# Tile loads on one DMA queue, tables on another, groups of 8, 7 and 9 tiles, and a conversion in five stages

## Chip, cores and metric

One core of one Trainium2 chip. The metric is the device time in microseconds (us) of one execution of the whole program.

## What is computed

Three parts follow each other on 3072 tokens of 512 features.

```python
for t in range(S):                                   # attention: B=4, H=8, S=768, D=64
    state = gamma * state + k[t] outer v[t]          # per batch and head, 64x64
    y[t] = scale * q[t] @ state
logits = x @ w_gate                                  # mixture of 8 experts, one per token
e = argmax(logits)
out = softmax(logits)[e] * sigmoid(x @ w_output_gate)[e] * (relu(x @ w1[e]) @ w2[e])   # 512 -> 1024 -> 512
h = x @ w_in                                         # dense part: 512 -> 2048 -> 512
out = (h - tanh(h)) @ w_out
```

All inputs are float32, but `w_in` and `w_out` reach the kernel as float64 (pairs of 32-bit words) and are converted on the chip. The matrix products of the experts and of the dense part are made of three products each: every float32 operand x is split into a rounded part `hi` and a rest `lo = x - hi`, and hi*hi, hi*lo, lo*hi are added.

## The kernel before, in words

The instructions are written in the order in which each engine runs them; the tile framework only adds the waits. So the order of the work is the order of the calls below, engine by engine, and an instruction that waits holds up all behind it on its engine or its DMA queue.

**Attention and gating** (loop over `n`, lines 914 to 995). 24 tiles of 128 tokens, six per batch. `load(n)` (L586) brings q, k, v of a tile (1 MB) by DMA; tiles 0 to 2 and 6 on are issued on SP, tiles 3, 4 and 5 on ScalarE's queue (ACT). Tables (`ca`: masks, powers and indices; `cb`: identity and indices; `wgs`: gate weights; `qt[1]`) come on SP between the first loads. At tile 6's load four stores of `lead` and one of `far` fill the pads of two DRAM tensors. Loads run up to five tiles ahead, from six buffers, later three tiles ahead from four. Per tile: `attend(n)` (L655: state, outputs `o`, on TensorE; copies `st`, `xT` on ACT), `scores(n + 2)` (L617: products `sc`, masked on VectorE as `pt`; `qd`, `kd` on GpSimd), `rows(n)` (L705: transposes `tr`, copies `xr` on ACT, row sums `lp` on VectorE, and a store of `xr` to the DRAM tensor `xtok`, issued on ACT).

Tiles form three groups of eight. At a group's end VectorE picks each token's expert (`onehot`), TensorE counts ranks (`ranks`), VectorE writes for each tile a mark of 432 columns (`ohr`, L799) and computes gates (`scale`); these short operations wait in lists, `scales` and `convs`, and `fill` (L325) lets a budget of 2.6 (an estimate in us) of them onto VectorE per tile, each costed at 0.2 if it names no other figure. `slots` (L853) then gathers the places of tokens by products `ip`. After the second group, `head` (L864) gathers the first 216 tokens of expert 0 from the tiles so far; so steps of that expert can begin as attention ends.

**Conversion of float64** (`conv_m`, L264). A piece is half of one of 16 blocks of weights, 128x512 values: ACT copies the high words (`keep`), VectorE makes exponent and mantissa (`ta`, `va`, five operations, v0 to v4), ACT rounds to `hi`, GpSimd subtracts for `lo` (L308). 32 pieces in all; four (NPA) are converted in attention through the list `convs`, 28 in the places of the experts. Blocks 12 to 15 (NRES on) go back to DRAM (`dh`, `dl`) and are read again in the last stage.

**Experts** (place 0 from L1003, the other places in the loop at L1099). Nine places: two halves of expert 0 (216 tokens each), then seven experts in the order of their counts, with 432, 420, 408, 400, 388, 380 and 368 columns. Each place has eight steps `i`: `mm1` (L417, TensorE product `ph`, then `hi` on ACT and `lo` on VectorE) and `mm2` of the step before (L434, product `ya`). The weights of the next step (`wr`, 0.5 MB by SP, three buffers) are split into `wh` on ACT and `wl`, by `conv_w` (L231): part 0, for `mm1`, on VectorE in odd steps and on GpSimd in even ones, part 1, for `mm2`, on VectorE. Tokens of the next place are gathered by GpSimd (`gather`), scaled by ACT (`weigh`) and transposed and split (`turn`, `split`: `xt`, `xh`, `xl`), in steps 6 and 7 of a place, two transposed blocks in each. One slot of the conversion falls into most steps: a slot with the third stage of piece j - 1 (ACT `hi`, GpSimd subtraction) and the first of piece j (ACT `keep`, VectorE v0 to v2), then a slot with the second of piece j (v3, v4).

**Last stage.** Six blocks of 512 tokens (`fetch2`, `split2`: DMA `x2r` from DRAM, `x2h` on ACT, `x2l` on GpSimd; block 0's are issued in the last place), 16 steps each of `mm3` and `mm4` (L1200, L1214).

## Time and profile before

| | us |
|---|---|
| median of 3 runs | 1029.43 |
| lowest and highest of them | 1029.24, 1035.13 |
| the profiled execution | 1026.86 |
| its span, first to last instruction | 1025.1 |
| TensorE busy in the span | 972.1 |

The profile is of one execution. PE is TensorE's products, PEld its weight loads, DVE VectorE, ACT ScalarE, POOL GpSimd, SP the engine that only issues DMAs; a q behind an engine's name (ACTq) is its sequencer, which issues DMAs and waits. L308 is line 308 of the kernel. A tile's name stands left of the arrow where it is written and right of it where it is read. A bracket at a line's end is the idle time of the engine before that instruction and what ended it. The granted clock is that of TensorE, 1.00 for 2.4 GHz.

### The profile page before, as it was taken

Reading aid. Unit: us, or ns where it says so; the run is one execution under the profiler, and the core shown is the slowest. Engines: PE = TensorE matmul, PEld = TensorE weight load, DVE = VectorE, ACT = ScalarE, POOL = GpSimd, SP = SyncE. Lnnn points to the kernel's source line nnn. Section 1 sums busy time; section 2 is a strip of 40 time slices with the busy share of each in tenths; the row PEclk is TensorE's granted clock in tenths of the full one; section 3 lists DMA queues with packets and bytes.
Section 4 is the critical chain, followed back from the end, with each engine's and each line's share of the span. In section 5 each row is a group of like instructions: output and inputs, shape, how many; then the busy total and the mean of one; then the engine's idle time right before and its main releaser. Section 6 shows DMA issues by size and latency. Waiting matters only on the chain.

```text
span 1025.1 us, 16478 instructions
## 1 busy us (share of the span) xinstructions
PE 972.1 (95%) x5938; PEld 837.6 (82%) x5938; DVE 744.6 (73%) x1181; ACT 604.0 (59%) x1090; POOL 379.1 (37%) x333
## 2 busy tenths in 40 slices
PE   6899788999999999999999999999999999999995
PEld 4778678898989898999888888888888888888884
DVE  2387775778787788674987777777777777777772
ACT  2444342555565655554877767676676767767662
POOL 3276433243343353322342343243334325333322
PEclk9899998999999999999999999999999999999998
DMA  9899534476666675675300010010001001000001
GB/s 331 286 370 336 197 108 127 143 231 194 206 197 202 188 244 180 217 229 157 131 22 11 11 52 14 9 52 21 11 14 50 22 1 52 11 1 21 21 1 44
DMA packets 44011, 120.70 MB, mean 118 GB/s; under 512 B 9638, under 2 KB 15014, under 8 KB 41106
## 3 DMA queue, kind: packets, MB, share of 16 engines
q1 hardware_dynamic: 35170, 97.23, 29.1%
q0 software_dynamic: 4864, 12.91, 3.9%
q10 hardware_dynamic: 3888, 9.44, 2.4%
q8 instruction: 48, 0.79, 0.3%
q14 instruction: 41, 0.34, 0.1%
HBM read 95.99 MB, written 23.57 MB: 117 GB/s over the span
## 4 chain that ended last, share of the span: by engine, by line
PE 78%; DVE 9%; issue 4%; DMA 4%; ACT 2%; POOL 2%; SPq 0%; ACTq 0%; POOLq 0%; DVEq 0%
PE mh L1200 26%; PE ma L1214 26%; PE ph L427 9%; PE ya L451 9%; PE tr L716 2%; PE sc L631 1%; DMA x2c<-lead 1%; DVE ta L278 1%; DVE va L281 1%; PE o L690 1%; DVE wl L239 1%; DMA xtok<-xr 1%; DVE pt L624 1%; POOL wl L239 1%; DMA ld<-in_qkv 1%
## 5 line engine op out<-in xcount | busy, mean ns | idle before, releaser
L1182 POOL TENSOR_TENSOR gl<-g,gh 128x512 fp32r<-128x512 f32 x96 | 124.1, 1293 | 343.7 <-ACT gh L1181 341.1
L1200 PE MATMUL mh<-x2h,ml 128*128 128x512 f32 x384 | 151.6, 395 | 0.0
L1214 PE MATMUL ma<-ml,gh 128*128 128x512 f32 x384 | 151.6, 395 | 0.0
L1200 PE MATMUL mh<-x2h,mh 128*128 128x512 f32 x384 | 151.6, 395 | 0.0
L1214 PE MATMUL ma<-mh,gl 128*128 128x512 f32 x384 | 151.3, 394 | 0.0
L1214 PE MATMUL ma<-mh,gh 128*128 128x512 f32 x384 | 150.9, 393 | 0.0
L1200 PE MATMUL mh<-x2l,mh 128*128 128x512 f32 x384 | 150.9, 393 | 0.0
L1175 DVE COPY_PREDICATED g<-big,td 128x512 f32<-128x512 int32 x96 | 143.3, 1492 | 9.9
L1165 DVE SCALAR_TENSOR_TENSOR g<-s,mh 128x512 f32<-128x512 f32 x96 | 65.8, 686 | 101.6 <-ACT s L1163 86.9
L1161 ACT ACTIVATE u<-mh 128x512 f32<-128x512 f32 x96 | 57.6, 600 | 128.0 <-PE mh L1200 123.7
L237 ACT ACTIVATE wh<-wr 128x512 fp32r<-128x512 f32 x136 | 83.6, 626 | 82.1 <-PE ya L451 75.0
L427 PE MATMUL ph<-xh,wl 128*128 128x216 f32 (+7 forms) x288 | 97.7, 339 | 10.6 <-DVE wl L239 7.9
L427 PE MATMUL ph<-xh,wh 128*128 128x216 f32 (+7 forms) x288 | 97.5, 339 | 0.6 <-ACT wh L237 0.6
L427 PE MATMUL ph<-xl,wh 128*128 128x216 f32 (+7 forms) x288 | 95.9, 333 | 1.3 <-DVE xl L407 1.3
L239 DVE TENSOR_TENSOR wl<-wr,wh 128x512 fp32r<-128x512 f32 x98 | 71.5, 731 | 34.2 <-ACT wh L237 33.5
L451 PE MATMUL ya<-lo,wh 128*128 128x216 f32 (+7 forms) x288 | 95.7, 332 | 0.3 <-DVE lo L431 0.3
L451 PE MATMUL ya<-hi,wh 128*128 128x216 f32 (+7 forms) x288 | 95.7, 332 | 0.0
L451 PE MATMUL ya<-hi,wl 128*128 128x216 f32 (+7 forms) x288 | 95.3, 331 | 0.0
L1200 PEld LDWEIGHTS mh<-x2l,mh 128*128 128x128 f32 x384 | 72.1, 188 | 17.3
L1200 PEld LDWEIGHTS mh<-x2h,ml 128*128 128x128 f32 x384 | 72.1, 188 | 17.2
L1214 PEld LDWEIGHTS ma<-mh,gh 128*128 128x128 f32 x384 | 72.1, 188 | 17.0
L1214 PEld LDWEIGHTS ma<-ml,gh 128*128 128x128 f32 x384 | 72.1, 188 | 17.0
(182 smaller groups left out, 2017.9 us busy)
## 6 DMA issues: line engine op xcount, KB each, us to landing
wr<-in_w SPq DMA_DIRECT2D x68, 512.0 KB
ld<-in_qkv SPq DMA_DIRECT2D x19, 1024.0 KB
m<-in_w SPq DMA_DIRECT2D x32, 512.0 KB
xtok<-xr ACTq DMA_DIRECT2D x24, 256.0 KB
x2r<-x2c SPq DMA_DIRECT2D x24, 256.0 KB
ld<-in_qkv ACTq DMA_DIRECT2D x3, 1024.0 KB
dh<-keep SPq DMA_DIRECT2D x8, 256.0 KB
dl<-ta SPq DMA_DIRECT2D x8, 256.0 KB
```

What stands on the lines that cost most here:

```text
L237: nc.scalar.activation(hi, t[:, cs], AF.Copy)
L239: eng.tensor_tensor(out=lo, in0=t[:, cs], in1=f32(hi), op=ALU.subtract)
L278: V.tensor_scalar(mcv[j]["ta"], mcv[j]["keep"], 4, 1, op0=ALU.logical_shift_left, op1=ALU.logical_shift_right)
L427: nc.tensor.matmul(ph, a[:, cs], b[:, kk, 0:ns], start=(k == 0), stop=(k == 3 * KD - 1))
L451: nc.tensor.matmul(accs[p][dk], a[:, cs], b, start=(k == 0 and j == 0 and (p > 0 or dk % 2 == 0)), stop=(k == NFE - 1 and j == 2), skip_gr ...
L716: nc.tensor.matmul(tr[:, j], xk, turn_rhs[:, kk], start=True, stop=True)
L1161: nc.scalar.activation(u, h, AF.Square)
L1165: nc.vector.scalar_tensor_tensor(out=g, in0=s1, scalar=PB1, in1=h, op0=ALU.add, op1=ALU.mult)
L1175: nc.vector.copy_predicated(g, big.bitcast(I32), td)
L1182: nc.gpsimd.tensor_tensor(out=lo, in0=g, in1=f32(hi), op=ALU.subtract)
L1200: nc.tensor.matmul(h, a[:, cs], c, start=(k == 0), stop=(k == 3 * KD - 1))
L1214: nc.tensor.matmul(macc[b][t], a[:, cs], c[:, DM:2 * DM], start=(f == 0 and j == 0), stop=(f == NFM - 1 and j == 2))
```

## The change

Tile loads are all issued on SP, loads 4 and 5 behind a small memset on VectorE that writes into their buffers. The tables are issued on ACT, the masks in two transfers instead of four, except a last part of `ca` that stays on SP behind load 4. Groups have 8, 7 and 9 tiles, with buffers by parity; a mark is costed at 0.35; the float64 pieces in attention are five. The conversion of a piece has five stages instead of three, each in a slot of its own, one slot per step from step 13 on, and the subtraction is on VectorE. Part 0 of the expert weights is split on GpSimd in every step of the later places, and on VectorE in place 0. Gathers, scalings and transposes of the next place have new steps, and x2 of the last stage's first block is fetched and split two parts at a time, after the last slot.

```diff
@@ -48,12 +48,12 @@
 PRE = TB - NS
 NPAD = PRE + N + NS
 NV = 5 * E
-GROUPS = (8, 8, 8)
+GROUPS = (8, 7, 9)
 TA = sum(GROUPS[:2])
 MOST = 2.6
 FAR = 1.0e6
 PG = P + 2 * E
-NPA = 4
+NPA = 5
 NRES = 12
 SCALE = 1.0 / float(D) ** 0.5
 
@@ -70,11 +70,11 @@
 
 C_MASK = 0
 C_K = C_MASK + H * P
-C_IOTA = C_K + (NCH - 1) * H
-C_TILE = C_IOTA + NS
+C_TILE = C_K + (NCH - 1) * H
 C_W8 = C_TILE + NT
 C_STEP = C_W8 + E
-C_Q = C_STEP + NPAIR
+C_IOTA = C_STEP + NPAIR
+C_Q = C_IOTA + NS
 NCONA = C_Q + NPAIR * P
 B_ID = 0
 B_TRI = B_ID + P
@@ -305,15 +305,17 @@
         def rest():
             t = mcv.pop(j)
             hi, lo = t["hl"]
-            nc.gpsimd.tensor_tensor(out=lo, in0=f32(t["va"]), in1=f32(hi), op=ALU.subtract)
+            V.tensor_tensor(out=lo, in0=f32(t["va"]), in1=f32(hi), op=ALU.subtract)
             if f >= NRES:
                 stores.append(lambda: nc.sync.dma_start(wdram[f][0][:, cs], f32(hi)))
                 stores.append(lambda: nc.sync.dma_start(wdram[f][1][:, cs], f32(lo)))
 
         return [
-            [("A", begin), ("V", v0), ("V", v1), ("V", v2)],
+            [("A", begin)],
+            [("V", v0), ("V", v1), ("V", v2)],
             [("V", v3), ("V", v4)],
-            [("A", high), ("P", rest)],
+            [("A", high)],
+            [("V", rest)],
         ][stage]
 
     stores = []
@@ -330,7 +332,7 @@
                 ops.pop(0)[1]()
 
     def piece(j, cv_p):
-        return [(*op, 0.65) for stage in range(3) for op in conv_m(j, stage, cv_p)]
+        return [(*op, 0.65) for stage in range(5) for op in conv_m(j, stage, cv_p)]
 
     wres, wdram = {}, {}
     for f in range(NRES, NFM):
@@ -406,13 +408,11 @@
         nc.scalar.activation(hi, tr, AF.Copy)
         nc.vector.tensor_tensor(out=lo, in0=tr, in1=f32(hi), op=ALU.subtract)
 
-    def turn(p, half):
-        ks = range(half * KD // 2, (half + 1) * KD // 2)
-        if len(chunks(p)) == HEAD:
-            split(p, list(ks))
-        else:
-            for kk in ks:
-                split(p, [kk])
+    def turn(p, kk):
+        if len(chunks(p)) > HEAD:
+            split(p, [kk])
+        elif kk % 2:
+            split(p, [kk - 1, kk])
 
     def mm1(i):
         p, f = steps[i]
@@ -583,7 +583,7 @@
                 cs = slice(hp * P, (hp + 1) * P)
                 nc.scalar.activation(qt[c][:, cs], qt[c - 1][:, cs], AF.Copy, scale=ca[:, C_STEP + hp:C_STEP + hp + 1])
 
-        def load(n, eng=nc.sync):
+        def load(n):
             if n < EARLIER and n % 6 >= 4:
                 t = ldb_p.tile([P, 4, DM], F32, tag="ld", name=f"ld{n}")
             else:
@@ -591,27 +591,25 @@
             if n == 0:
                 for half in (slice(0, DM // 2), slice(DM // 2, DM)):
                     nc.sync.dma_start(t[:, 0:2, half], qkv[n, :, 0:2, half])
-                for g in range(2):
-                    nc.sync.dma_start(ca[:, g * DM:(g + 1) * DM], cona[:, g * DM:(g + 1) * DM])
-                nc.sync.dma_start(ca[:, C_K:C_IOTA], cona[:, C_K:C_IOTA])
-                nc.sync.dma_start(ca[:, C_W8:], cona[:, C_W8:C_Q])
-                nc.sync.dma_start(t[:, 2:4], qkv[n, :, 2:4])
-            elif n == 1:
-                nc.sync.dma_start(t[:, 0:2], qkv[n, :, 0:2])
+                for cs in (slice(0, DM), slice(DM, C_IOTA)):
+                    nc.scalar.dma_start(ca[:, cs], cona[:, cs])
                 nc.sync.dma_start(t[:, 2:4], qkv[n, :, 2:4])
             else:
-                eng.dma_start(t, qkv[n])
+                if n in (4, 5):
+
+                    nc.vector.memset(t[:, 0, 0:1], 0.0)
+                nc.sync.dma_start(t, qkv[n])
             if n == 1:
-                nc.sync.dma_start(cb, conb)
-                nc.sync.dma_start(wgs, wg)
+                nc.scalar.dma_start(cb, conb)
+                nc.scalar.dma_start(wgs, wg)
             if n == 4:
-                nc.sync.dma_start(ca[:, C_IOTA:C_W8], cona[:, C_IOTA:C_W8])
+                nc.sync.dma_start(ca[:, C_IOTA:C_Q], cona[:, C_IOTA:C_Q])
             if n == NCH:
                 for kk in range(KD):
                     nc.sync.dma_start(x2c[kk, :, 0:PRE], lead)
                 nc.sync.dma_start(tokc[0:PRE].unsqueeze(0), far)
             if n == 1:
-                nc.sync.dma_start(qt[1], cona[:, C_Q:C_Q + DM])
+                nc.scalar.dma_start(qt[1], cona[:, C_Q:C_Q + DM])
             loaded[n] = t
 
         def scores(n):
@@ -725,7 +723,7 @@
 
         def group(gi, G):
             def gt(name, *shape, dtype=F32):
-                return gp.tile([P, G, *shape], dtype, tag=name, name=f"{name}{gi}")
+                return gp.tile([P, G, *shape], dtype, tag=f"{name}{gi % 2}", name=f"{name}{gi}", bufs=1)
 
             gst[gi] = dict(
                 lp=gt("lp", 2, 2 * E), lg=gt("lg", 2 * E), m=gt("m"), dl=gt("dl", E), t1=gt("t1", E), z=gt("z", E),
@@ -803,7 +801,7 @@
                 if later is None:
                     mark()
                 else:
-                    later.append(("V", mark))
+                    later.append(("V", mark, 0.35))
             if G > 1:
                 add = gp.tile([P, E], F32, tag="add", name=f"add{gi}_{g0}")
                 nc.vector.reduce_sum(out=add, in_=oh.rearrange("p g e -> p e g"), axis=AX.X)
@@ -903,7 +901,7 @@
         scores(1)
         nc.vector.tensor_copy(tri, cb[:, B_TRI:B_TRI + P])
         load(2)
-        load(3, nc.scalar)
+        load(3)
         nld = 4
         decay(2)
         J0 = 2 * NFM - NPA
@@ -922,9 +920,9 @@
                 flush()
                 rooms()
             while nld < NT and nld <= n + (5 if nld < EARLIER + 4 else 3):
-                load(nld, nc.scalar if nld < 6 else nc.sync)
+                load(nld)
                 nld += 1
-            if n >= TA - 1:
+            if n == TA or nld == NT:
                 feed()
             flush()
 
@@ -955,10 +953,13 @@
             after, soon = soon, []
 
             q = n - (NT - 7)
-            if 0 <= q < 4:
+            if 0 <= q < 3:
                 conv_w(q, 0)
-            if 1 <= q < 5:
+            if 1 <= q < 4:
                 conv_w(q - 1, 1)
+            if n == NT - 2:
+                conv_w(3, 0)
+                conv_w(3, 1)
             cuts = [0, G - 3, G - 1] if final else [0, G]
             if g + 1 in cuts[1:]:
                 g0 = cuts[cuts.index(g + 1) - 1]
@@ -978,8 +979,8 @@
                             head()
                             for k in range(2):
                                 due.setdefault(now[0] + 2, []).append(lambda k=k: weigh(0, k))
-                            for k in range(2):
-                                due.setdefault(now[0] + 2 + k, []).append(lambda k=k: turn(0, k))
+                            for kk in range(KD):
+                                due.setdefault(now[0] + 2 + kk // 2, []).append(lambda kk=kk: turn(0, kk))
 
                     def place(a=a, hi=hi, settle=settle):
                         ranks(*a, scales)
@@ -1031,7 +1032,7 @@
             gather(1, c)
         run(sc[7:])
         mm1(2)
-        conv_w(4, 0)
+        conv_w(4, 0, nc.vector)
         mm2(1)
         slots(gi, 0, G, 2 * E, NV)
         conv_w(4, 1)
@@ -1040,19 +1041,20 @@
         nc.vector.tensor_tensor(out=first_s, in0=first_s, in1=idxf[:, :, 2 * E:3 * E], op=ALU.add)
         for i in range(3, NFE):
             if i == NFE - 1:
-                for c in chunks(1):
-                    weigh(1, c)
-                for half in range(2):
-                    turn(1, half)
+                for kk in range(KD):
+                    turn(1, kk)
             if i + 2 < NFE:
-                conv_w(i + 2, 0)
+                conv_w(i + 2, 0, nc.vector)
             mm1(i)
             mm2(i - 1)
             if i + 2 < NFE:
                 conv_w(i + 2, 1)
                 feed()
             if i < 7:
-                (order, order, order, order)[i - 3](i - 3)
+                order(i - 3)
+            if i == 5:
+                for c in chunks(1):
+                    weigh(1, c)
         mm2(NFE - 1)
 
 
@@ -1083,26 +1085,23 @@
     NSTEP = len(steps)
     NPIECE = 2 * NFM - NPA
     CONV = NFE + NFE // 2 + 2
-    slots_m, nslot = [], 0
+
+    def stage(j, s):
+        return [lambda: run(conv_m(j, s, cv_p))] if 0 <= j < NPIECE else []
+
+    slots_m = [stage(0, 0)]
     for j in range(NPIECE + 1):
-        ops = []
-        if j:
-            ops.append(lambda j=j: run(conv_m(j - 1, 2, cv_p)))
-        if j < NPIECE:
-            ops.append(lambda j=j: run(conv_m(j, 0, cv_p)))
-        slots_m.append(ops)
-        if j < NPIECE:
-            ops = [lambda j=j: run(conv_m(j, 1, cv_p))]
-            if j + 2 < NPIECE:
-                ops.append(lambda j=j: load_m(j + 2, cv_p))
-            slots_m.append(ops)
+        slots_m.append(stage(j, 1) + stage(j - 1, 3))
+        slots_m.append(stage(j - 1, 4) + stage(j, 2) + stage(j + 1, 0))
+        if j + 2 < NPIECE:
+            slots_m[-1].append(lambda j=j: load_m(j + 2, cv_p))
     for i in range(NFE, NSTEP + 1):
         p, k = divmod(i, NFE)
         feed()
         flush()
         nxt = i + 1 if i + 1 < NSTEP and i + 1 in loads else None
         if nxt:
-            conv_w(nxt, 0, nc.vector if nxt % 2 else nc.gpsimd)
+            conv_w(nxt, 0)
         if i < NSTEP:
             mm1(i)
         if i > NFE:
@@ -1111,34 +1110,35 @@
             conv_w(nxt, 1)
         if p + 1 < NPL:
             for c in range(NCC):
-                if k == ((0, 0, 1, 1) if p == 1 else (0, 1, 2, 3))[c]:
+                if k == (0, 0, 1, 1)[c]:
                     gather(p + 1, c)
-                if k == ((3, 3, 4, 4) if p == 1 else (2, 3, 4, 5))[c]:
+                if k == ((3, 3, 4, 4) if p == 1 else (2, 2, 3, 3))[c]:
                     weigh(p + 1, c)
-            if k >= NFE - 2:
-                turn(p + 1, k - (NFE - 2))
+            if k >= NFE - KD:
+                turn(p + 1, k - (NFE - KD))
         if NFE <= i < NFE + 5:
             table(i - NFE)
         if i == CONV - 2:
             whl2_p.release()
             cv_p = tc.alloc_tile_pool(name="cv", bufs=1, side="right", reuse_waits="tile")
-            cv_bufs[cv_p] = dict(keep=2, ta=2, va=2)
+            cv_bufs[cv_p] = dict(keep=3, ta=2, va=2)
             load_m(0, cv_p)
             load_m(1, cv_p)
-
-        while nslot < len(slots_m) and nslot * (NSTEP - NFE + 2 - CONV) < len(slots_m) * (i - CONV + 1):
-            for op in slots_m[nslot]:
+        if CONV - 1 <= i < CONV - 1 + len(slots_m):
+            for op in slots_m[i - CONV + 1]:
                 op()
-            nslot += 1
-        if i == NSTEP - NFE + 2:
+        if i == CONV - 2 + len(slots_m):
+            flush()
             cv_p.release()
             for name in ("pk", "gx"):
                 ep.pop(name).release()
             x2_p = ctx.enter_context(tc.tile_pool(name="mx2", bufs=8, reuse_waits="tile"))
-        if i < NSTEP and p == NPL - 1 and 3 <= k < 3 + KD:
-            fetch2(0, k - 3)
-        if i < NSTEP and p == NPL - 1 and 4 <= k < 4 + KD:
-            split2(0, k - 4)
+        late = 2 * (i - (CONV - 2 + len(slots_m)))
+        for kk in (late, late + 1):
+            if 0 <= kk < KD:
+                fetch2(0, kk)
+            if 0 <= kk - 2 < KD:
+                split2(0, kk - 2)
 
     for name in ("ye", "hh", "xs"):
         ep.pop(name).release()
```

## Rows read from the trace of the kernel before

**Rows 1.** The page: busy time of each engine, share of the span, instructions
```profile
PE 972.1 (95%) x5938; PEld 837.6 (82%) x5938; DVE 744.6 (73%) x1181; ACT 604.0 (59%) x1090; POOL 379.1 (37%) x333
```

**Rows 2.** Stretches: length; busy PE, PEld, DVE, ACT, POOL (count); clock, DMA share, GB/s
```profile
0.00:50.00 50.00, 36.26 (x446) 29.47 (x446) 15.58 (x42) 15.50 (x39) 14.43 (x28) 0.90 0.86 308
50.00:100.00 50.00, 48.08 (x766) 41.39 (x766) 39.88 (x106) 21.77 (x53) 35.58 (x48) 1.00 0.96 348
100.00:140.00 40.00, 32.69 (x480) 28.11 (x480) 32.10 (x98) 16.59 (x39) 18.78 (x22) 0.96 0.60 211
140.00:180.00 40.00, 34.48 (x323) 33.26 (x316) 25.59 (x92) 10.94 (x28) 11.54 (x10) 0.91 0.32 96
180.00:478.70 298.70, 286.12 (x1636) 273.05 (x1635) 230.25 (x363) 167.23 (x316) 111.20 (x86) 0.99 0.62 197
478.70:1013.20 534.50, 534.50 (x2304) 432.31 (x2302) 400.45 (x482) 371.99 (x618) 186.03 (x139) 1.00 0.10 30
```

**Rows 3.** Waits: engine and line, waited for; us in total, times, longest
```profile
ACT st L684 <- DMA x2c<-lead: 10.8, 1, 10.8
...
PE ph L427 <- DVE wl L239: 7.9, 9, 2.0
...
PE ph L427 <- POOL wl L239: 2.5, 4, 1.2
```

**Rows 4.** Timeline of the first 60 us: start, duration, instruction [idle before]
```profile
17.73 0.63 ACT L719 ACTIVATE xr<-tr 128x256 f32<-128x256 f32 x2
...
28.76 0.34 ACTq L724 DMA_DIRECT2D xtok<-xr  x1
...
30.07 2.29 PE L716 MATMUL tr<-turn_rhs,xT 128*128 128x144 f32 x8 [6.09 <-ACT xT L699]
```

**Rows 5.** Chain that ended last, 0 to 200 us: start, duration, what
```profile
14.13 14.55 DMA x2c<-lead
```

**Rows 6.** Timelines of VectorE and TensorE, 108 to 142 us
```profile
117.55 4.32 DVE L799 TENSOR_SCALAR ohr<-iota,rank 128x432 bf16<-128x432 f16 x8
...
122.52 2.65 PE L631 MATMUL sc<-ld 64*128 64x128 f32 x16 [3.66 <-DVE pt L624]
...
130.65 1.16 PE L631 MATMUL sc<-ld 64*128 64x128 f32 x16
```

**Rows 7.** Timelines of VectorE, GpSimd and TensorE, 149 to 180 us
```profile
152.60 3.21 DVE L842 CAST part<-s 128x8 bf16<-128x8 f32 x1
...
153.28 2.48 POOL L239 TENSOR_TENSOR wl<-wr,wh 128x512 fp32r<-128x512 f32 x2
...
156.12 2.06 PE L859 MATMUL ip<-ohv,ohr 128*108 128x24 bf16 x32 [3.61 <-DVE ohv L846]
```

**Rows 8.** Groups by line, 180 to 478.7 us: busy, mean ns; idle before, releaser
```profile
L239 DVE TENSOR_TENSOR wl<-wr,wh 128x512 fp32r<-128x512 f32 x90 | 65.6, 731 | 34.0 <-ACT wh L237 33.5
...
L278 DVE TENSOR_SCALAR ta<-keep 128x512 uint32<-128x512 uint32 x28 | 28.4, 1014 | 18.1 <-ACT keep L275 18.1
...
L239 POOL TENSOR_TENSOR wl<-wr,wh 128x512 fp32r<-128x512 f32 x30 | 42.7, 1423 | 64.6 <-ACT wh L237 64.6
L308 POOL TENSOR_TENSOR ml<-va,mh 128x512 fp32r<-128x512 f32 x24 | 31.3, 1302 | 91.8 <-ACT mh L303 91.8
...
L237 ACT ACTIVATE wh<-wr 128x512 fp32r<-128x512 f32 x120 | 74.3, 626 | 80.1 <-PE ya L451 75.0 <-DMA wr<-in_w 4.6
...
L391 ACT ACTIVATE gx<-gx,sslot 108x512 f32<-108x512 f32 (+6 forms) x28 | 19.7, 710 | 0.0
```

**Rows 9.** Chain that ended last, 350 to 480 us
```profile
408.65 2.84 PE ph L427 x11
...
419.28 2.17 PE ph L427 x11
```

**Rows 10.** Timeline of GpSimd, 455 to 484 us, and the whole chain
```profile
475.74 1.29 POOL L1080 TENSOR_TENSOR x2l<-x2r,x2h 128x512 fp32r<-128x512 f32 x1 [0.56 <-ACT x2h L1079]
...
478.67 14.01 PE mh L1200 x60
```

## Prediction

> **What bounds the kernel now.** I read the page's busy times first: TensorE is busy 95% of the span [rows 1]. A share over the whole span hides stages with different limits, so next I cut the span at the stage borders [rows 2]. The last stage, 478.7 to 1013.2 us, has TensorE busy for all of its 534.5 us at full clock; the change touches only what comes before, and behind it come only the last stores. TensorE's idle time, span less busy, can be recovered only before 478.7: 13.7 us in 0 to 50, 1.9 in 50 to 100, 7.3 in 100 to 140 (attention), 5.5 in 140 to 180 (first place of the experts), 12.6 in 180 to 478.7 (the other places); 41 us in all. The third view is the list of waits [rows 3], which says what ends this idle time: at the start one wait of ScalarE for the landing of the `lead` stores, in the places VectorE's `wl`, nine times, and GpSimd's `wl`, four times. The fourth is the timeline around each of these waits.
>
> The profiled execution took 1026.86 us, 1.76 more than its span. The sum below is made against it; the median of the runs, 1029.43, is 2.57 higher, and I add that at the end.
>
> **Start: loads on SP, tables on ACT, memsets ahead of loads 4 and 5.** xr of tile 0 is done at 17.73 + 0.63 = 18.4 us, and its store leaves ACT only at 28.76 [rows 4], when the `lead` store, issued at 14.13 on SP behind whole tiles, has landed at 28.68 [rows 5]. The store reads nothing of it; the wait is an order between DMAs. For 10.3 us ACT does nothing behind that store, and TensorE's transposes of tile 1 wait 6.09 us for ACT's xT (30.07). The change takes loads 3, 4, 5 off ACT and gives it five tables, which are issued before its first activation; that is free, ACT has nothing else to do then. SP loses eight issues and gains three loads; loads 6 on and the four `lead` stores stay behind them. With fewer large loads before it, the store can leave at 18.4 at best, and at 28.7 at worst, if it must wait for a landing behind loads again: -10.3 to 0. The memsets sit on VectorE behind the first two tiles' masks and delay loads 4 and 5 to about 17 us, which tile 4 doesn't feel before tile 1 is through. DMA was busy 86% of the first 50 us, so 7 us of it lay unused, which is the room for earlier loads. I take -8, nearer to the full wait because it is one wait, whose cause (large loads on ACT's queue) is gone.
>
> The Trainium skill ("DMA: Bandwidth & Descriptors", section "Issuing engines are not separate DMA queues") says that DMAs from different engines run on the same 16 DMA engines, and that a second issuer saves only issue time. By that alone this term would be near 0 and the sum 8 us higher; the row shows a wait of ACT, not of bandwidth, so I go by the row.
>
> **Fifth piece of the conversion in attention, its subtraction on VectorE.** From 50 to 100 us VectorE is busy 39.9 us and DMA 96% [rows 2]. A piece more is five VectorE operations of 0.7 to 1.0 us (`ta` has a mean of 1.01 [rows 8]) and the subtraction, 0.73 by the `wl` of the same shape: 4.2 to 5.7 us, and the subtractions of the four other pieces 4 x 0.73 = 2.9. That makes 7 to 8.6 us on an engine with 10 us free there, in order, ahead of the masks that TensorE needs. DMA gets 1.05 MB more, 3.0 us at 348 GB/s. Bounds 0 (all in VectorE's gaps) to +7 (all late). GpSimd's four subtractions of 1.30 go. I take +2.
>
> **Groups of 8, 7, 9 and the weight 0.35 of a mark.** At 117.55 us eight marks stand on VectorE for 4.32 us; the masks queue behind them, and TensorE waits 3.66 us (122.52) and then runs 16 score products in 2.65 us, where a set that waits for nothing takes 1.16 (130.65) [rows 6]. With the mark's price at 0.35 instead of 0.2 the budget of 2.6 per tile takes four or five of them there, and group 1 closes a tile earlier, so that the head's gather is off the end. Conversion of expert step 3 moves to tile 22. Bounds -6 (the wait, the slow set and the later 1.2 us) to 0. I take -3.5; what is late next is the last group's own chain.
>
> **First place, 140 to 180.** A conversion of eight columns took 3.21 us on VectorE (152.60 to 155.81), ending with two GpSimd `wl` (153.28 to 155.76), and TensorE waited 3.61 us for it [rows 7]. These two `wl` go to VectorE, behind the chain: 2 x 0.73 after the point where TensorE is released. The scaling of the next place's tokens is issued a whole step ahead of its transposes. Of the 5.5 us idle there, bounds -6 (with the lower clock, 0.91) to -1; I take -4.
>
> **Places of the experts, 180 to 478.7.** Today one step holds ACT's `mh` and `keep`, and VectorE's `ta`, `va`, `ta` on that same `keep`; VectorE waits 18.1 us for `keep` over 28 pieces, and `wl` of every other step stands behind it in the same queue [rows 8]. Spaced, `keep` is a step old when VectorE comes to it. The exchange on the engines is even: VectorE loses 30 `wl` (21.9 us at 0.731) and gains 27 subtractions (19.7); GpSimd loses 28 subtractions (36.5) and gains 30 `wl` (42.7). What goes is the waits: 12.6 us idle, and slow products after the longest (11 in 2.84 us, against 2.17 two steps on [rows 9]), some 1.5 us with the second half of that step. Bounds -14 to 0 here (above 0 is the first rival); I take -11, because the longest waits all end on VectorE's `wl`.
>
> The Trainium skill ("SBUF — State Buffer", section "Who interferes with whom") has VectorE and GpSimd exclude each other for a whole instruction where both read two SBUF inputs. By that each new subtraction can lose a whole GpSimd `wl`, 1.42 us, or 27 x 1.42 = 38 us of VectorE, and this term would be near 0. No row shows it at that rate: VectorE's own `wl`, the same form, has a mean of 0.73 while GpSimd is busy 37% of the stage.
>
> **Scaling and transposes in the places.** Both scalings of a pair now stand in one step (2 x 0.71 on ACT), and a place's transposes are one per step from the fifth on. In the place of rank 0's second half the last scalings are in the very step of the first transposes: TensorE waits there for `wh` and two scalings, 0.63 + 1.42 = 2 us once [rows 8]. Bounds 0 to +4 (with slow products behind it as in [rows 9]); I take +2.
>
> **Border to the last stage.** Conversion ends in step 69 instead of 65, and x2 is fetched and split two at a time, behind the last piece's stores on SP. Today the last x2l ends at 477.03, 1.6 us before the first product of the last stage at 478.67 [rows 10]. In the change fetches 2 and 3 wait for splits 0 and 1 (two buffers), one GpSimd operation of 1.29 and one landing later. Bounds 0 to +5; I take +2.5.
>
> **Sum.** -8 + 2 - 3.5 - 4 - 11 + 2 + 2.5 = -20.0. Against the profiled execution 1006.9, against the median 1029.43 - 20 = 1009.4. All favourable ends together give -36, all unfavourable ones +15.
>
> **Rivals.**
> 1. *GpSimd's `wl` is late in every step (slower).* ACT's `wh` stands behind two scalings, GpSimd takes 1.42 where VectorE takes 0.73, and TensorE's second product needs it. Today's four waits for it average 2.5 / 4 = 0.62 us [rows 3]. At 60 steps that is 37.5 us in place of the 12.6: the places' term is +25 instead of -11, the time 1045. It outweighs the other gains of 9 us from (12.6 + 9) / 60 = 0.36 us a step. For: the shorter steps of the last places. Against: today only 4 of 30 were waited for, with a 1.30 us subtraction ahead of them in the same queue, which goes.
> 2. *The start gives nothing:* the first store waits for another large load that came before it. 1029.43 - 12 = 1017.4. For: the `lead` stores stay where they are, behind loads 4, 5, 6. Against: the store is free to leave before them. The page named above has the same outcome.
> 3. *VectorE becomes the bound of attention:* +7 instead of +2, and 0 for the groups: 1009.4 + 8.5 = 1018. For: 80% busy there already, 10 us free. Against: GpSimd's operations beside it become fewer.
> 4. *The spacing doesn't free `wl`,* or two of these together: the places' term -3 and the start's 0, 1009.4 + 16 = 1025: the change doesn't do what it says, and the median stays within 1%.
>
> **How the numbers follow.** Chances: forecast 0.51, rival 1 0.07, rival 2 0.17, rival 3 0.13, rival 4 0.12. Faster by over 1% (under 1019.1; 1% is about what a measurement of this kernel can tell from no change) is the forecast but for 0.02 of it, and of rivals 2 and 3, which lie just under that line, two thirds: 0.49 + 0.20 = 0.69. Slower by over 1% (over 1039.7) is most of rival 1: 0.06. The rest, 0.25, is within 1%. The range leaves out the best tenth (-32.5, the starts and places both near their ends) and, above, rival 1 and the worst of rival 4: 997 to 1028.
>
> **What would show it.** Right: the store of tile 0 leaves before 22 us; no wait of ACT for `lead`; TensorE's idle time in the places under 5 us, none of its waits ending on VectorE's `wl`; no 3 us conversion beside GpSimd at the end of attention; one wait of about 2 us in rank 0's second place and one at the border. Wrong: waits of TensorE for GpSimd's `wl` in most steps; VectorE over 95% busy from 50 to 100 us with score products waiting for its masks; the first store after 27 us.

## The result, and the profile after

| us | before | after |
|---|---|---|
| median (4 runs each) | 1029.58 | 1018.27 |
| lowest and highest | 1029.24, 1035.13 | 1016.71, 1020.13 |
| profiled execution | 1026.86 | 1016.71 |
| its span | 1025.1 | 1014.9 |
| TensorE busy in it | 972.1 | 969.5 |

The ratio is 0.9878, with an interval of 0.9839 to 0.9917: 0.8 to 1.6% faster, 11.3 us by the medians where 20 were forecast. The forecast of 1009.4 is missed by 8.9, inside its range and on its side.

The first view to read after a change in many stages is a table by stage, of points that every kernel has: the first `o` product that reads the masked scores `pt` of tiles 2, 18 and 23, the first `ph` of expert steps 0, 3, 8 and 70, and the first `mh` of the last stage, in us from the start of each profiled execution. Most of the experiments told of below stand with them. Each row is one execution, and TensorE's granted clock, which differs between executions, is in it: where it matters, it is said.

| kernel | tile 2 | tile 18 | tile 23 | step 0 | step 3 | step 8 | step 70 | last stage | end | 8 to 70 | 70 to last stage |
|---|---|---|---|---|---|---|---|---|---|---|---|
| before | 34.3 | 108.2 | 140.1 | 141.1 | 158.0 | 178.2 | 468.4 | 478.5 | 1025.1 | 290.3 | 10.1 |
| after | 23.2 | 99.4 | 135.7 | 136.8 | 154.2 | 169.9 | 452.9 | 466.4 | 1014.9 | 283.0 | 13.4 |
| e1 queues only | 23.0 | 99.5 | 132.0 | 133.1 | 151.0 | 171.0 | 461.4 | 471.5 | 1017.7 | 290.4 | 10.1 |
| e2 four pieces | 23.1 | 99.7 | 132.3 | 133.3 | 156.1 | 171.8 | 461.8 | 473.9 | 1023.5 | 290.0 | 12.1 |
| e3 old turns | 23.0 | 97.6 | 133.3 | 134.3 | 155.5 | 171.2 | 450.3 | 462.3 | 1012.9 | 279.1 | 12.0 |
| e5 unspaced | 23.5 | 97.4 | 133.5 | 134.5 | 152.0 | 167.7 | 449.7 | 459.7 | 1007.4 | 282.0 | 10.1 |
| e6 conversion first | 23.1 | 104.6 | 129.8 | 130.9 | 149.6 | 165.3 | 448.6 | 460.7 | 1010.1 | 283.3 | 12.1 |
| e9 old groups | 23.1 | 98.2 | 136.1 | 137.1 | 156.9 | 174.2 | 458.3 | 470.4 | 1020.3 | 284.1 | 12.1 |
| e11 old engines | 23.0 | 98.0 | 134.7 | 135.8 | 156.2 | 174.9 | 451.8 | 461.9 | 1010.8 | 276.9 | 10.1 |
| e12 three edits | 23.1 | 100.0 | 132.8 | 134.7 | 148.5 | 165.8 | 442.6 | 452.7 | 1001.4 | 276.8 | 10.1 |

The windows of the changed kernel, with the columns of [rows 2], cut at its own stage borders:

```profile
0.00:50.00 50.00, 42.68 (x535) 33.90 (x537) 20.31 (x54) 18.99 (x47) 24.30 (x42) 0.93 0.91 336
50.00:100.00 50.00, 48.62 (x796) 42.37 (x794) 43.57 (x138) 20.74 (x53) 22.88 (x32) 1.00 0.95 363
100.00:136.80 36.80, 25.61 (x382) 21.93 (x378) 26.56 (x67) 15.42 (x33) 17.27 (x20) 0.86 0.54 185
136.80:169.90 33.10, 29.89 (x292) 29.24 (x291) 23.63 (x94) 10.05 (x25) 6.64 (x7) 0.95 0.42 124
169.90:453.00 283.10, 274.84 (x1592) 263.74 (x1591) 224.20 (x350) 161.86 (x305) 106.66 (x83) 1.00 0.63 199
453.00:470.00 17.00, 15.21 (x74) 13.68 (x73) 5.17 (x7) 5.89 (x11) 6.36 (x5) 0.90 0.33 95
```

TensorE's idle time, length less busy, fell from 13.7 to 7.3 us in the first 50, and is now largest at the end of attention: 11.2 us of 36.8. TensorE's list of waits says by what:

```profile
PE tr L714 <- ACT xT L697: 13.2, 3, 9.3
PE ph L427 <- POOL wl L239: 6.3, 10, 0.9
...
PE ya L451 <- ACT hi L430: 1.6, 1, 1.6
...
PE ya L451 <- DVE lo L431: 1.3, 1, 1.3
```

VectorE's `wl`, TensorE's first wait in [rows 3], is gone from the list; GpSimd's `wl` has gone from four waits and 2.5 us to ten and 6.3; and one wait of 9.27 us is new. ScalarE's timeline shows the start (the store stood at 28.76 in [rows 4]) and a new wait of its own:

```profile
17.73 0.63 ACT L717 ACTIVATE xr<-tr 128x256 f32<-128x256 f32 x2
18.39 0.34 ACTq L722 DMA_DIRECT2D xtok<-xr  x1
...
38.89 0.66 ACT L275 ACTIVATE keep<-m 128x512 f32<-128x512 f32 x1 [5.27 <-DMA m<-in_w]
```

The store leaves 10.4 us earlier, as soon as `xr` is there. The new wait of 9.27 us stands in the timeline of the three engines at tile 18:

```profile
100.30 3.64 DVE L797 TENSOR_SCALAR ohr<-iota,rank 128x432 bf16<-128x432 f16 x5
...
103.86 1.09 DVE L296 TENSOR_TENSOR va<-va,ta 128x512 f32<-128x512 f32 x1
104.98 0.63 ACT L303 ACTIVATE keep<-va 128x512 fp32r<-128x512 f32 x1 [4.54 <-DVE va L296]
...
106.71 0.69 DVE L281 SCALAR_TENSOR_TENSOR va<-keep,ta 128x512 uint32<-128x512 uint32 x1
...
109.40 0.63 ACT L303 ACTIVATE keep<-va 128x512 fp32r<-128x512 f32 x1 [3.23 <-DVE va L296]
...
110.20 0.59 ACT L697 ACTIVATE xT<-o 128x512 f32<-128x512 f32 x1
...
110.84 2.29 PE L714 MATMUL tr<-turn_rhs,xT 128*128 128x144 f32 x8 [9.27 <-ACT xT L697]
```

At tile 18 the buffers of the attention's conversion are given up, so the code runs all that is left of it (`run(convs)`): 11 operations, counted in the list of fill work as the program builds it. They pass between ACT and VectorE, behind five marks, and ACT's `xT`, for which TensorE waits, is queued behind them. Before, nothing was left: no operation of the conversion stands at that point of its timeline.

The groups of the places, as [rows 8]:

```profile
L239 DVE TENSOR_TENSOR wl<-wr,wh 128x512 fp32r<-128x512 f32 x58 | 41.3, 712 | 28.5 <-ACT wh L237 27.7
...
L239 POOL TENSOR_TENSOR wl<-wr,wh 128x512 fp32r<-128x512 f32 x59 | 81.3, 1378 | 171.1 <-ACT wh L237 165.8 <-PE ph L427 5.3
...
L278 DVE TENSOR_SCALAR ta<-keep 128x512 uint32<-128x512 uint32 x27 | 20.0, 741 | 3.2 <-DMA dl<-ta 3.2
...
L308 DVE TENSOR_TENSOR ml<-va,mh 128x512 fp32r<-128x512 f32 x24 | 16.4, 683 | 0.0
```

VectorE no longer waits for `keep` (18.1 us before). Its 3.2 us ahead of `ta` are one wait, for the landing of the store that still reads that buffer. And at the border, the timeline of the stores, the fetches and the last step:

```profile
456.30 0.32 SPq L311 DMA_DIRECT2D dl<-ta  x1
...
458.17 6.43 SPq L1074 DMA_DIRECT2D x2r<-x2c  x4
...
461.04 1.33 ACT L1081 ACTIVATE x2h<-x2r 128x512 fp32r<-128x512 f32 x2 [3.23 <-DMA x2r<-x2c]
...
462.27 0.46 ACT L430 ACTIVATE hi<-ph 128x368 fp32r<-128x368 f32 x1
...
462.78 0.43 PE L451 MATMUL ya<-hi,wh 128*128 128x368 f32 x1 [1.62 <-ACT hi L430]
```

The fetches stand behind the last piece's store of `ml` (456.30) in SP's queue, x2h waits for them, and the last step's relu `hi` stands behind x2h on ACT.

### The profile page after: what moved, and what is told of

Read it like the earlier page. It is cut to its first block, busy times and chain, and to the rows that moved or that the text cites. A ratio compares the mean times of both kernels' runs of the same rounds, so it can differ in the third digit from the quotient of the medians.

```text
span 1014.9 us, 16466 instructions
## 1 busy us (share of the span) xinstructions
PE 969.5 (96%) x5942; PEld 834.8 (82%) x5942; DVE 746.1 (74%) x1189; ACT 604.8 (60%) x1090; POOL 371.5 (37%) x327
## 4 chain that ended last, share of the span: by engine, by line
PE 75%; DMA 10%; DVE 7%; ACT 3%; issue 1%; POOL 1%; SPq 1%; ACTq 0%; POOLq 0%; DVEq 0%
PE ma L1214 26%; PE mh L1200 25%; PE ph L427 8%; PE ya L451 7%; DMA wr<-in_w 5%; PE tr L714 2%; PE sc L629 1%; PE o L688 1%; DMA qt<-in_cona 1%; DMA ld<-in_qkv 1%; DVE ta L291 1%; PE xt L404 1%; ACT wh L237 1%; DMA x2c<-y 1%; DVE ta L278 1%
## 5 line engine op out<-in xcount | busy, mean ns | idle before, releaser
L239 POOL TENSOR_TENSOR wl<-wr,wh 128x512 fp32r<-128x512 f32 x64 | 87.7, 1370 | 203.5 <-ACT wh L237 185.7
L1214 PE MATMUL ma<-mh,gh 128*128 128x512 f32 x384 | 151.0, 393 | 0.1
L1214 PEld LDWEIGHTS ma<-mh,gl 128*128 128x128 f32 x384 | 72.1, 188 | 17.5 <-POOL gl L1182 1.1
L1214 PEld LDWEIGHTS ma<-mh,gh 128*128 128x128 f32 x384 | 72.1, 188 | 17.5 <-ACT gh L1181 0.6
L1200 PEld LDWEIGHTS mh<-x2h,mh 128*128 128x128 f32 x384 | 72.2, 188 | 17.3 <-DVE td L1174 0.5
```

The source lines that it names most:

```text
L239: eng.tensor_tensor(out=lo, in0=t[:, cs], in1=f32(hi), op=ALU.subtract)
L1200: nc.tensor.matmul(h, a[:, cs], c, start=(k == 0), stop=(k == 3 * KD - 1))
L1214: nc.tensor.matmul(macc[b][t], a[:, cs], c[:, DM:2 * DM], start=(f == 0 and j == 0), stop=(f == NFM - 1 and j == 2))
```

## The experiments

The differences by stage, after less before, are -11.1 at tile 2, +2.3 from there to tile 18, +4.4 from 18 to 23, -3.9 from 23 to step 8, -7.2 from step 8 to 70, and +5.3 to the end. Theory after this reading: the start and the spacing do what they should, and the run at tile 18 and the border give half of it back. The experiments take the parts one by one. The medians are of four to six runs, except where it is said, each beside runs of the kernel before on the same chip (medians 1030.3 to 1031.1).

**e1: the queues alone.** The kernel before, with the new `load` (its loads on SP, its tables on ACT) and the order of the constants, nothing else.

> The kernel before with the DMA part of the change alone (loads on SP, tables on ACT, the two memsets). Theory (a wait of ACT was removed): the first store leaves ACT before 20 us, tile 2's output products start near 23 us as in the changed kernel (34.3 before), and most of these 11 us reach the end of attention, since four pieces leave nothing to run at tile 18: first expert product at 141.1 - 8 = 133 us, time about 8 us under before. Rival (the 16 DMA engines set the pace, not the queue): the 11 us are lost again between 50 and 100 us, first expert product within 2 us of 141.1, time within 2 us of before.

1023.64 us, ratio 0.9938 (0.9915 to 0.9962). Tile 2 comes at 23.0 and step 0 at 133.1, 8.0 earlier than before. From there on the kernel is as before: the two waits of [rows 6] and [rows 7] stand there still, some 8 us earlier on the timeline of TensorE:

```profile
113.90 2.67 PE L629 MATMUL sc<-ld 64*128 64x128 f32 x16 [3.66 <-DVE pt L622]
...
148.06 1.11 PE L857 MATMUL ip<-ohv,ohr 128*108 128x24 bf16 x11 [3.60 <-DVE ohv L844]
```

So the start's term is real, and step 0 is here 3.7 us earlier than in the whole change: what the change adds to attention costs more than its groups save. Of the 11.3 us at tile 2, 8.7 are left at tile 18: some 2.6 are lost on the way, with nothing but the queues changed. Loads, tables and memsets were moved together; which of them counts was not tried apart.

**e2: four pieces in attention.** The 28th piece goes back to the places, into the slots there are.

```
-NPA = 5
+NPA = 4
+    slots_m = (slots_m[:8] + [slots_m[8] + slots_m[9]] + slots_m[10:17]
+               + [slots_m[17] + slots_m[18]] + slots_m[19:])
```

> The changed kernel with four pieces in attention, the 28th in the places (two steps there run two slots). Theory (the fifth piece doesn't fit into the budget and is run in one chain of ACT and VectorE at tile 18, in front of attention's copies): TensorE's wait of 9.27 us at 110.8 falls under 4 us, tile 19 starts 5 to 8 us earlier, time 5 to 8 us under the changed kernel, 1010 to 1013. Rival (VectorE's total work bounds attention): the wait comes back in smaller waits from 50 to 130 us, the first expert product gains at most 2 us of the 0.7 + 2.9 us of VectorE work taken out, time within 3 us of the changed kernel.

1019.0, ratio 0.9889 (0.9867 to 0.9910), no gain on the change. The wait at tile 18 fell to 4.85 us (three operations are left), and step 0 came 3.5 us earlier; but the places took 7 us more, and steps 0 to 3 took 22.8 us instead of 17.4, at a granted clock of 0.63 (the last section comes back to this). That the doubled slots cost the 7 us is not shown: near the end of the places VectorE waited 5.31 us for the landing of the store of its `ta` buffer, 3.17 in the change, and TensorE behind it 4.18 us instead of 1.32; the products after it ran at the lower clock (0.51 us against 0.33).

```profile
445.62 0.68 PE L451 MATMUL ya<-lo,wh 128*128 128x368 f32 x1 [4.18 <-DVE lo L431]
```

**e3: the old turns.** Gathers, scalings and transposes of the next place in the steps of before.

```
-                if k == (0, 0, 1, 1)[c]:
+                if k == ((0, 0, 1, 1) if p == 1 else (0, 1, 2, 3))[c]:
...
-                if k == ((3, 3, 4, 4) if p == 1 else (2, 2, 3, 3))[c]:
+                if k == ((3, 3, 4, 4) if p == 1 else (2, 3, 4, 5))[c]:
...
-            if k >= NFE - KD:
-                turn(p + 1, k - (NFE - KD))
+            if k >= NFE - 2:
+                for kk in range(2 * (k - NFE + 2), 2 * (k - NFE + 2) + 2):
+                    turn(p + 1, kk)
```

> The changed kernel with gathers, scalings and transposes of the places in their old steps. Theory (two scalings in one step push ACT's wh, and with it GpSimd's wl, past its due time in steps 3 and 4 of each place): the waits of TensorE for GpSimd's wl (6.3 us in all) fall under 2 us, and the places (169.9 to 453.0, steps 8 to 70) get 4 to 8 us shorter. Rival (GpSimd's 1.37 us a wl is too slow as such): the waits stay above 4 us and turn up in steps 6 and 7 too; the places change by less than 2 us.

1014.59, ratio 0.9846 (0.9812 to 0.9880): the places take 279.1 instead of 283.0, and TensorE's waits for GpSimd's `wl` there fall from 6.3 us to 3.0, not under 2. In the change all ten of these waits stand in steps 3 and 4 of a place, behind the paired scalings; in e3 five are left. So with two scalings in one step, ACT's next `wh` is late, and GpSimd's `wl`, 1.38 us long, has no slack left.

**e4: those `wl` on VectorE.** `conv_w(nxt, 0, nc.vector if nxt % NFE in (3, 4) else None)`.

> The changed kernel with part 0 of the weights of steps 3 and 4 of each place split on VectorE instead of GpSimd (14 of 60 conversions). Theory (ACT's queue is late by the scalings, GpSimd adds only 0.7 us): the waits move to VectorE's wl and shrink by about half; the places gain 2 to 5 us. Rival (GpSimd's speed alone is the cause): TensorE's waits for wl vanish and the places gain 8 us or more.

1017.71, ratio 0.9859 (0.9834 to 0.9883); the places 284.9, no gain in all. The waits for GpSimd went; TensorE's list for the places has in their stead:

```profile
PE ph L427 <- DVE wl L239: 6.2, 8, 4.5
PE ph L427 <- ACT wh L237: 2.0, 3, 1.2
```

The one of 4.54 us is for a `wl` that stands on VectorE behind a wait of 4.76 us for the landing of the store of `ta` (3.17 in the change). The other seven come to 1.7 us, and with the 2.0 for `wh` to a little over half of the 6.3 in the change, as the theory had it. So in these steps both count, the late `wh` and the longer `wl`; what this edit is worth alone, the run doesn't tell.

**e5: not spaced.** The change with the conversion's slots as before it.

```
-        slots_m.append(stage(j, 1) + stage(j - 1, 3))
-        slots_m.append(stage(j - 1, 4) + stage(j, 2) + stage(j + 1, 0))
+        slots_m.append(stage(j - 1, 3) + stage(j - 1, 4) + stage(j, 0) + stage(j, 1))
+        slots_m.append(stage(j, 2))
```

> The changed kernel, with the float64 conversion in the places issued as before the change: the closing pair of a piece and the opening pair of the next (`keep` and `ta`, `va`, `ta`) in one expert step; the engines (subtraction on VectorE, `wl` on GpSimd) stay as changed. Theory (the spacing is what freed the places): VectorE waits 12 to 20 us for ACT's `keep` and `hi` of the conversion over the places, the stretch from expert step 8 to step 70 grows from 283.0 us to 288 or more, and the median from 1018.3 to 1022 or more. Rival (taking `wl` off VectorE did it, and the spacing adds nothing): the stretch stays within 2 us of 283.0 and the median within 2 us of 1018.3.

1012.14, ratio 0.9832 (0.9796 to 0.9869), against my theory. The median is below the change's, though the intervals of the two ratios overlap. The places take 282.0, with the clock at its lower level from 328.0 to 331.5 us, so beside the new engines the spacing adds nothing, as the rival said. VectorE waits 6.0 us for `mh` and not at all for `keep`, where the theory had 12 to 20: its own subtraction now stands ahead of `ta` in the queue, and `keep` is done by then; and the border is back at 10.1, since a piece's last two stages share a slot and the conversion ends a step earlier. TensorE's waits from step 8 to 70 are the same kind as after the change, seven of them:

```profile
PE ph L427 <- POOL wl L239: 5.5, 7, 1.0
```

**e6: conversion ahead of the scalings.** All five pieces are issued before tile 18.

```
-            fill([scales, convs], MOST - busy)
+            fill([scales, convs] if n < 9 else [convs, scales], MOST - busy)
...
-        return [(*op, 0.65) for stage in range(5) for op in conv_m(j, stage, cv_p)]
+        return [(*op, 0.5) for stage in range(5) for op in conv_m(j, stage, cv_p)]
```

> The changed kernel, with the conversion ahead of the gate's scalings in the list of fill work from tile 9 on, and priced 0.5 instead of 0.65 an operation, so that all five pieces are issued before tile 18 and nothing is left for the run at tile 18. Theory (the 11 operations run there, a chain of ACT and VectorE, are the wait of TensorE of 9.27 us): that wait falls under 3 us, the first product of expert step 0 comes at 128 to 131 us instead of 136.8, the median falls to 1010 to 1013. Rival (VectorE has no room for the fifth piece anywhere in attention, it is busy 43.6 of 50 us between 50 and 100): the same time comes back as waits for masks between tiles 9 and 18, tile 18 starts 5 us later or more than at 99.4, and step 0 at 134.5 or later.

1010.72, ratio 0.9815 (0.9768 to 0.9862). The wait of 9.27 is gone, none over 1 us stands at tile 18, and step 0 comes at 130.9, 5.9 us earlier. Part of it moved, as the rival had it: tile 18 starts 5.2 us later than in the change. The run at tile 18 was the wait, and some 6 of its 9 us were avoidable.

**e7: products in a gap.** Eight products of ones where TensorE stands 2.06 us for the split of the head's tokens, in step 0.

```
+            if i == 0 and k == 8:
+                warm(8)
```

> The changed kernel, with eight products of ones added into an unused bank in expert step 0, at the point where TensorE stands still for 2.06 us for the split of the head's tokens. Theory (the lower clock in the first expert steps, granted 0.90 in the profile of the change and 0.62 to 0.68 in three experiments with the same code there, comes from TensorE's standing still ahead of it, and it is why the end of attention gained less in most executions than in the profiled one): granted clock 0.95 or more from step 0 to step 3, these steps take 17.5 us or less, and the median falls by 3 to 4 us to about 1015. Rival (the clock falls for another reason, or for the earlier waits at 131 and 134 us): granted clock under 0.9 again, 20 us or more, and a median within 2 us of 1018.3.

1017.02, ratio 0.9860 (0.9831 to 0.9888), as the change. The gap is filled, as TensorE's timeline shows:

```profile
137.16 1.90 PE L196 MATMUL warm<-ones 128*128 128x512 bf16 x8
139.38 0.37 PE L429 MATMUL ph<-xl,wh 128*128 128x216 f32 x1 [0.32 <-DVE xl L409]
```

The clock falls all the same: steps 0 to 3 take 17.4 us at 0.90, as in the profile of the change. The time is inside the theory's 17.5, but so was the change's; the clock and the median are as the rival had them. What this run shows is that filling this gap doesn't keep the clock up; the earlier waits that the rival names were not tried.

**e8: the border, and a third `ta`.** The last two slots in one, and `ta=3`.

```
+    slots_m[-2:] = [slots_m[-2] + slots_m[-1]]
...
-            cv_bufs[cv_p] = dict(keep=3, ta=2, va=2)
+            cv_bufs[cv_p] = dict(keep=3, ta=3, va=2)
```

> The changed kernel, with two small edits that are read in two places. The last two slots of the conversion are one, so that it ends an expert step earlier and the fetches of x2 start a step earlier; and the conversion's `ta` has three buffers instead of two. Theory: the border (first product of step 70 to the first of the last stage) falls from 13.4 to about 10.5 us, as before the change, since the wait of 1.62 us for ACT's relu queued behind x2h goes; and TensorE's wait of 1.32 us at 447 us goes, where VectorE's `ta` stood 3.17 us for the landing of the store of the same buffer. Median 1013 to 1015. Rival: the fetches wait for the stores ahead of them in SP's queue whenever they start, two buffers for x2r still put fetches 2 and 3 behind splits 0 and 1, and the border stays at 12.5 us or more; and the third buffer only moves the wait to `keep`. Median within 2 us of 1018.3.

1020.89, ratio 0.9897 (0.9869 to 0.9925). The third buffer took away the wait of 1.3 us for `lo`. The fetches start 0.2 us after step 70 begins instead of 5.3, and yet the border got worse, 15.4 us (at a granted clock of 0.89): x2h and x2l, waiting for the fetches, now stand ahead of the last step's `wh` and `wl`, on TensorE's timeline:

```profile
465.94 0.43 PE L427 MATMUL ph<-xh,wl 128*128 128x368 f32 x1 [2.56 <-POOL wl L239]
```

**e9: the old groups and the old price of a mark.** `GROUPS = (8, 8, 8)`, and `("V", mark)`.

> The changed kernel with the groups of before (8, 8, 8) and the mark's price of before (0.2); everything else as changed. Group 1 then ends at tile 15, and by the list of fill work 3 conversion operations instead of 11 are left for the run at tile 18. Theory (groups and price took away the clump of marks, and thereby brought in the longer run at tile 18): TensorE's wait at tile 18 falls from 9.27 to about 4.9 us, as with four pieces; a wait of 3 to 4 us for marks and slow score products come back before tile 23; step 0 comes at 135 to 139 us against 136.8, and the median stays within 2.5 us of 1018.3: this part of the change gives and takes about the same. Rival (the clump was of no account once the loads start earlier): no wait over 2 us between tiles 19 and 23, step 0 at 133 or earlier, and a median of 1015 or less.

1022.34 (six runs, 1014.93 to 1025.32), ratio 0.9893 (0.9850 to 0.9935). TensorE's timeline has both waits, as the theory had it: 3 operations are left at tile 18, and the clump of marks is back.

```profile
105.47 2.29 PE L714 MATMUL tr<-turn_rhs,xT 128*128 128x144 f32 x8 [5.16 <-ACT xT L697]
...
118.56 2.20 PE L629 MATMUL sc<-ld 64*128 64x128 f32 x16 [3.58 <-DVE pt L622]
```

Step 0 comes at 137.1 against 136.8. The median is 4 us over the change's, more than the theory allowed, with runs 10 us apart; steps 0 to 8 took 37.1 us in its profiled execution instead of 33.1, at a lower clock. In this company the groups and the price move the wait from tile 20 to tile 18. That they pay when the run at tile 18 is gone too is likely from e6, whose step 0 is 2.2 us ahead of e1's, but no run has e6 with the old groups.

**e11: the old engines.** The conversion spaced as changed, but in the places its subtraction on GpSimd, and every other step's first `wl` on VectorE.

```
+            sub = V if j >= 2 * NFM - NPA else nc.gpsimd
-            V.tensor_tensor(out=lo, in0=f32(t["va"]), in1=f32(hi), op=ALU.subtract)
+            sub.tensor_tensor(out=lo, in0=f32(t["va"]), in1=f32(hi), op=ALU.subtract)
...
-            conv_w(nxt, 0)
+            conv_w(nxt, 0, nc.vector if nxt % 2 else nc.gpsimd)
```

> The changed kernel with the conversion spaced in five stages as changed, but in the places the engines of before: the conversion's subtraction on GpSimd, and every other step's first `wl` on VectorE. With the unspaced kernel this gives the four corners: before 290.3 us from expert step 8 to step 70 (old engines, not spaced), after 283.0 (new engines, spaced), unspaced 282.0 (new engines, not spaced). Theory A, as predicted before the run of the change (the wait of VectorE for `keep` held up its `wl`, and spacing removes that wait): 281 to 285 us here too, TensorE waits for VectorE's `wl` under 2 us in all. Theory B (only the exchange of the engines helps, since any VectorE `wl` behind the conversion's chain comes late, spaced or not): 288 us or more, and six or more waits of TensorE of over 0.6 us for VectorE's `wl`.

1006.93, ratio 0.9746 (0.9703 to 0.9790): 11.3 us faster than the change. The four corners, step 8 to step 70:

| | wl by turns, subtraction on GpSimd | wl on GpSimd, subtraction on VectorE |
|---|---|---|
| not spaced | 290.3 (before) | 282.0 (e5) |
| spaced | 276.9 (e11) | 283.0 (after) |

By these corners each of the two helps without the other; the spacing without the exchange helps most; and the exchange on top of it costs 6.1 us. The last is one edit, with the clock at its upper level throughout in both. The others are not so clean: the corner of before has also the old turns, 28 pieces in the places instead of 27 and two `keep` buffers instead of three, and in before (409.9 to 413.3 us) and in e5 the clock was at its lower level for a while, worth up to 1.7 us each. The waits of TensorE in this stretch of e11 come to 3.6 us, where the change has 8.1 and before 12.4:

```profile
PE ph L428 <- DVE wl L239: 3.0, 6, 0.8
```

The border is the exchange's too, where the conversion is spaced: 12.0 to 12.1 us in e2, e3, e6, e7 and e9, at the upper clock throughout, 10.1 here. The change's own 13.4 has the lower clock in it from 463.6 us on (granted 0.90 in the last of its windows above). With the subtraction on GpSimd the last `ml` is stored at 451.56 us, before step 70 begins, as the timeline shows, and the fetches start 1.6 us after step 70 begins instead of 5.3:

```profile
451.56 0.32 SPq L312 DMA_DIRECT2D dl<-ta  x1
...
453.42 6.80 SPq L1075 DMA_DIRECT2D x2r<-x2c  x4
```

Theory B of the expectation falls. Theory A holds, and its 281 to 285 us were too cautious; of the waits for VectorE's `wl` 3.0 us are left where it had under 2.

**e10: e3, e5 and e6 together.**

> The changed kernel with three of the edits tried: conversion not spaced in the places, conversion ahead of the gate's scalings in attention at a price of 0.5, and the old turns of gathers, scalings and transposes. Alone they gave 1012.1, 1010.7 and 1014.6 us against 1018.3. Theory (they act in different stages, so the gains add: 6.2, 7.6 and 3.7 us): step 0 at about 131 us, the stretch from step 8 to step 70 under 280 us, the border about 10 us, the median 1000 to 1004. Rival (the border or the lower clock takes it back, or the old turns and the unspaced conversion meet in the same steps): the stretch stays at 282 or more, the median at 1007 or more.

1006.87, ratio 0.9732 (0.9675 to 0.9789); the places 277.4, the border 10.1, both as the theory had them. But step 0 came at 133.8 instead of 131: in the profiled execution ACT's first `keep` waited 5.76 us for its load, and tile 18 started at 107.6. The median lies between the theory's and the rival's. For the cause it says more than e11: this kernel keeps the exchange, and its places and its border are those of e11 within 0.6 us. So what the exchange costs depends on its company: 6.1 us with the paired scalings and the spacing, about nothing with neither.

**e12: old engines, conversion first, first piece two tiles later.** The diffs of e11 and e6, and `if n >= 6 and n % 2 == 0 and nconv < nload` in place of `n >= 4`.

> The changed kernel with the engines of before in the places (as in the run with old engines, 1006.9 us, 276.9 us from step 8 to step 70), with the conversion ahead of the gate's scalings from tile 9 on at a price of 0.5 (alone 1010.7 us), and with the first piece in attention begun at tile 6 instead of 4, so that ACT's first `keep` doesn't stand for the landing of its load (5.27 us in the changed kernel's profile, 2.11 in another execution with the same code there). Theory (three places, the gains add): no wait of ACT over 1 us for the first load of the conversion, tile 6 at 38 to 40 us, no wait of TensorE over 3 us at tile 18, step 0 at 127 to 130 us, 277 us from step 8 to 70, border 10 us, median 998 to 1002. Rival (attention has no room: conversion before tile 18 delays the masks by what the run at tile 18 cost): tile 18 at 104 us or later, step 0 at 132 or later, median 1004 or more.

1003.23 (five runs, 1002.81 to 1007.46), ratio 0.9748 (0.9722 to 0.9775): faster than both kernels, with an interval clear of the change's. Its ratio is that of e11 and e10, so among these three I claim no order. The places and the border are as expected, and no first `keep` waits. Tile 6, at 40.7, is a little late, and step 0 is not as expected: 134.7 instead of 127 to 130. The head's tokens are gathered as tile 22 starts and not tile 21, which I put down to the delayed scalings, and a new wait takes the place of the old one:

```profile
129.99 1.82 PE L405 MATMUL xt<-cb,gx 108*128 108x108 f32 x8 [5.46 <-DVE gx L390]
```

## Why the prediction came out as it did

- **Start, -8.** Measured -11.1 at tile 2, which is beyond the bound of -10.3, and -8.0 at step 0, where e1 shows it alone. The row of the wait was the right guide, and rival 2 is out. The Trainium skill's rule on issuers ("DMA: Bandwidth & Descriptors", "Issuing engines are not separate DMA queues") would have had the term near 0. The wait wasn't for bandwidth.
- **Fifth piece +2, groups and price -3.5: together -1.5, measured +3.7** (tile 23 and step 0, the change against e1). The stage differences, +2.3 and +4.4, make it look like +6.7, but e1, which has neither, has +2.6 and +0.6 of them too. This is the first step that failed: "A piece more is five VectorE operations ... I take +2". The volume was right, VectorE was busy 43.57 of 50 us from 50 to 100. Missed was the end: what the budget does not issue by tile 18 is run there, in a row, ahead of `xT`. The term was priced by an engine's free time, and its place was set by a deadline in the code. With four pieces step 0 is 3.5 us earlier (e2), with the old groups 0.3 later (e9): in this company the piece cost 3.5 instead of 2, and the groups gave 0.3 instead of 3.5. The clump of [rows 6] did go, as e9 shows by bringing it back. Without the run at tile 18 step 0 is 5.9 us earlier (e6), 2.2 ahead of e1. Rival 3 had the sign, by another mechanism.
- **First place, -4.** Measured -3.9, by the profiled executions, and in part by the clock. The wait of [rows 7] fell from 3.61 us to 0.67; a new one, 2.06 us for the split of the head's tokens, was 0.27 before. Steps 3 to 8 take 15.7 us in the change and in e2 to e8, 20.2 in before and 20.0 in e1; but these two had a granted clock of 0.85 and 0.86 there, the others 1.00, and e10 and e11, which have the move of `wl` off the chain, took 18.8 and 18.7 at 0.83. At a like clock the move is thus worth some 1.4 us; whether the wait brought the lower clock on is open. What steps 0 to 3 take varies with the clock too, and makes the term uncertain by up to 5 us.
- **Places, -11; scalings +2.** Measured -7.2 for both. Two steps failed together: "The exchange on the engines is even", and the place of the scalings' wait. The spacing without the exchange gave -13.4 (e11, with what else differs from before), more than the -11. The exchange then took 6.1 back, 4.5 of it in waits and the rest in slower products. The totals of busy time were even, as said; but `wl` stands between ACT's `wh` and TensorE, and there its length and not its sum counts: 1.38 us on GpSimd, 0.71 on VectorE. Two scalings ahead of `wh` used up the slack: the old turns alone get 3.9 us back (e3). That is the mechanism of rival 1, in ten of the 60 steps, 0.63 us each by the list of waits. The wait of 2 us that I expected for the scalings, in rank 0's second place, was 0.30; their cost came in steps 3 and 4 of the later places.
- **Border and last stage, +2.5.** Measured +5.3, 3.3 of it at the border. There the exchange costs 2.0 us (12.0 to 12.1 against 10.1), and the rest is the lower clock of this execution. So the price was about right. The fetches stand behind the last piece's store, as I had it; what I did not have is that VectorE's last subtraction makes this store late, and that TensorE's wait of 1.62 us is for the relu `hi` behind x2h on ACT, where I had fetches 2 and 3 behind the splits. The rest of the difference is in the last stage, and I have not followed it.
- **Sum.** e11 stands at 1006.9, close to the forecast of 1009.4, which had the exchange at nothing. That is in part chance: the run at tile 18 is still in e11, and the spacing gave more than forecast. The 11.3 us between the medians of e11 and the change are 6.1 and 3.3 by the stages, as far as one execution of each can say.
- **The signs that I named.** Right: the store at 18.4; no wait for `lead`; no wait on VectorE's `wl`; one wait at the border; no 3 us conversion beside GpSimd at 150. Wrong: 8.3 us of idle time in the places instead of under 5, and no wait of 2 us in rank 0's second place.

## What to carry to other kernels

When work is handed from one engine to another, compare not only the totals but the length of the one operation that stands between a producer and the engine that sets the end: a longer `wl` with an even balance cost some 6 us here where its producer was late, and next to nothing where the steps were arranged otherwise (e10). When background work is added to a stage, look in the code for the point at which what is left of it is run all at once. And of two remedies for one wait, try each alone, since here, by the stage table, one was worth more without the other.
